# Moving the tiles that transfers touch to the front of the on-chip buffer, each on a multiple of 256 bytes

## The chip, the cores and the metric

One core of a Trainium2 chip runs the kernel. The metric is the device time of one execution in microseconds. The kernel before takes 166.34 us, the median of three runs (165.75 to 167.51 us). The execution that was profiled took 166.82 us, of which 165.1 us lie between its first and its last instruction.

## The reference

The inputs r, k, v and w are arrays of 4 batches, 8 heads, 768 steps and 48 values per head, all float32. An attention with a decaying state runs over the steps, and its output goes through a feed-forward layer with an activation that is normalized twice:

```python
state = zeros((B, H, D, D))
for t in range(S):
    cur = einsum('bhd,bhe->bhde', u * k[t], v[t])
    y[t] = einsum('bhd,bhde->bhe', r[t], state + cur)
    state = w[t][..., None] * state + einsum('bhd,bhe->bhde', k[t], v[t])
x = y, as [3072, 384]
h = x @ w_in                              # 384 x 1024
solu = h * softmax(h)
ln = (solu - mean(solu)) / sqrt(var(solu) + 1e-6) * g_ln
out = ln @ w_out                          # 1024 x 384, float32
```

## The kernel before, in words

The 3072 tokens are cut into 24 units of 128 steps (six chunks of four batches). For each unit four loads bring in 128 rows of w, k, r and v. In memory the 48 float32 values of a step and a head lie side by side, which is 192 bytes, and the rows of a head follow one another; another head lies elsewhere. On chip a row (one partition) of a tile has 8 slots of 64 float32, of which 48 are filled. So a load of 192 KB is made of 1,024 pieces (128 partitions by 8 heads) of 192 bytes each, and the pieces of one partition begin 256 bytes apart. k and r of a unit share a tile `kr_in` of 4,096 bytes a partition; `w_in` and `v_in` have 2,048 each. There are seven buffers of each (`NIO`).

ScalarE then takes the logarithm of w (`lw`), TensorE sums it up over the steps (`cum`), ScalarE takes exponentials (`ex`), VectorE scales k and r (`kp`), TensorE transposes them (`krk`, `krr`), forms the scores (`M`), the output of the attention (`Y`) and the new state (`S`). GpSimd computes the bonus for the step itself (`p`, `q`, `dv`) and casts v (`vb`). The second half transposes y (`X`), multiplies it by w_in (`H`), takes exponential, product and square (`e`, `he`, `hq`), multiplies by w_out (`Oa`, `Ob`; the tile is `o_ps`), scales the rows (`o`) and stores them (`out`, 1,536 bytes a partition).

Both weight matrices are loaded as float32 into `win_f` (three loads of 512 KB) and `wout_f` (two loads of 768 KB, in pieces of 1,536 bytes) and turned into bf16 once. For w_out this is a chain: eight parts are multiplied by the gain (`gw`, seven of them on GpSimd), TensorE takes the column means (`mn`), and VectorE adds them (`ce`; the tile is `w2`, in the rows `w`). Only then can the first `Oa` run.

The order of the work on every engine is the order of the words in the string `ORDER`; each engine follows it strictly (`InOrder`), and so does the queue of SyncE (SP), which issues every load and every store. "hot" are matmuls on a tile of zeros. All instructions are issued by one line of that helper, so in the profile nearly all have line 87, and they are told apart by their tiles.

Tiles in the pool `consts` are allotted in the order in which the code makes them, one behind the other, each rounded up to 32 bytes a partition. Above them lie 16,384 bytes of a scratch area and four constants of 32 bytes each, so the first tile of the kernel begins at byte 16,512 of a partition.

Of the kernel before, what the change touches and what calls it, by code (L numbers as in the profile page):

```python
# [8 lines left out]
F32 = mybir.dt.float32  # L9
# [60 lines left out]
NIO, NLW, NKP, NWK = 7, 10, 6, 4  # L70
# [24 lines left out]
def kernel(  # L95
# [13 lines left out]
    B, H, S, D = r.shape  # L109
    C = 128  # L110
    NC = S // C
    DM = H * D
    DF = moe_w_in.shape[1]
    HP = H // 2
    KM = DM // 128
    KF = DF // 128
# [8 lines left out]
    consts = ctx.enter_context(tc.tile_pool(name="consts", bufs=1))  # L125
    psum = ctx.enter_context(tc.tile_pool(name="psum", bufs=1, space=bass.MemoryType.PSUM))

    def ring(name, n, shape, dtype):
        return [consts.tile(shape, dtype, name=f"{name}{j}") for j in range(n)]
# [2 lines left out]
        return psum.tile(shape, dtype, tag=slot, name=name)  # L132


    warm = consts.tile([128, 512], BF16)
    dve.memset(warm, 0.0)
    uti_neg = consts.tile([C, C], BF16)
# [31 lines left out]
    ones_row = consts.tile([1, C], F32)  # L169
    dve.memset(ones_row, 1.0)  # L170

    w_t = ring("w_in", NIO, [C, H, 64], F32)
    kr_t = ring("kr_in", NIO, [C, 2, H, 64], F32)
    v_t = ring("v_in", NIO, [C, H, 64], F32)
    lw_t = ring("lw", NLW, [C, H, 64], BF16)
    kp_t = ring("kp", NKP, [C, 2, H, 64], BF16)
    for j in range(max(NLW, NKP)):
# [28 lines left out]
    qm_t = ring("qm", NWK, [C, 1], F32)  # L206
    lv_t = ring("lv", NWK, [C, 1], F32)
    rs_t = ring("rs", NWK, [C, 1], F32)
    o_t = ring("o", NWK, [C, DM], F32)

    u_row = consts.tile([1, DM], F32)
    g_rows = consts.tile([KF, 128], F32)
    u_bc = consts.tile([C, H, D], BF16)
    gr = consts.tile([128, KF], F32)
    win_f = consts.tile([128, KM, DF], F32)
    win_sb = consts.tile([128, KM, DF], BF16)
    wout_f = consts.tile([128, KF, DM], F32)
    mean_sb = consts.tile([128, DM], BF16)
    ps = {}

# [274 lines left out]
    def store(i, x):  # L495
# [10 lines left out]
        H=hidden, e=hidden_exp, he=hidden_mul, hq=hidden_square, Oa=output_a, Ob=output_b,  # L506
        sq=sums, qm=variance, lv=scale, o=scaled_out, out=store,
    )
    for word in ORDER.split():
        word, _, how = word.partition(".")  # L510
        name = word.rstrip("0123456789")
# [31 lines left out]
```

## Time and profile before

| what | value |
|---|---|
| median of three runs | 166.34 us |
| profiled execution | 166.82 us, span 165.1 us |
| TensorE (PE) busy | 142.1 us, 86% of the span |
| VectorE (DVE) busy | 130.6 us, 79% |
| ScalarE (ACT) busy | 119.1 us, 72% |
| GpSimd (POOL) busy | 102.7 us, 62% |
| TensorE's granted clock, mean | 0.969 of full |
| transfers | 27.08 MB in 104,825 packets, of which 100,313 under 512 bytes |

"Busy" is the time in which an engine has an instruction under way. The share of the transfer engines is the sum of the durations of all packets over 16 engines and the time; packets of one engine can overlap, so that it can go beyond 100%. SPq is the queue of SyncE: its rows are the times that it took to issue transfers, and waiting for room behind earlier transfers is inside them.

### The profile page before, as it was taken

To read this page: it belongs to the slowest core of one execution; us is meant where nothing else is said; L and a number is where in the kernel's file an instruction comes from. 1 tells how busy PE (TensorE), PEld (TensorE's weight loads), DVE (VectorE), ACT (ScalarE), POOL (GpSimd) and SP (SyncE) were. 2 spreads that over 40 slices of the span, in tenths; PEclk is the share of its full clock that TensorE was granted. 3 is DMA by queue.
4 is the path that set the end of the run, shared out by engine and by line. 5 is a ranking of instruction groups with operands and counts; after the bars stand their busy time and mean duration, and the time that the engine had idled before them with its cause. 6 is when DMAs were issued, how large, how long until landed. Compare 5 with 4: busy or idle time off the path is not lost.

```text
span 165.1 us, 5279 instructions
## 1 busy us (share of the span) xinstructions
PE 142.1 (86%) x2161; PEld 109.8 (67%) x2161; DVE 130.6 (79%) x227; ACT 119.1 (72%) x241; POOL 102.7 (62%) x131
## 2 busy tenths in 40 slices
PE   3789749158799999999999998998899789999990
PEld 1245438027578788887778787785778569798860
DVE  5054668364999999999889987996997899999553
ACT  3162775523779998899988979885979678665951
POOL 7340855996908999697759907999216893770000
PEclk9999999955899999999999999999999999999999
DMA  6999999999999999999999899999999931111023
GB/s 105 167 169 234 195 331 331 148 173 156 168 163 154 182 156 206 139 209 161 171 239 221 140 203 184 201 183 162 189 175 226 183 91 65 38 48 50 1 99 143
DMA packets 104825, 27.08 MB, mean 164 GB/s; under 512 B 100313, under 2 KB 104418, under 8 KB 104802
## 3 DMA queue, kind: packets, MB, share of 16 engines
q1 hardware_dynamic: 104802, 26.75, 92.0%
q8 instruction: 17, 0.28, 0.8%
q14 instruction: 6, 0.05, 0.2%
HBM read 22.03 MB, written 4.72 MB: 162 GB/s over the span
## 4 chain that ended last, share of the span: by engine, by line
PE 33%; DMA 21%; SPq 15%; POOL 10%; DVE 8%; ACT 6%; issue 4%; POOLq 0%; ACTq 0%
SPq L87 15%; PE o_ps L87 12%; PE h_ps L87 9%; DMA w_in<-in_w_dram 6%; DMA kr_in<-in_r_dram 6%; DMA wout_f<-in_moe_w_out_dram 5%; POOL w L87 5%; DMA v_in<-in_v_dram 4%; DVE w L87 3%; PE y_ps L87 3%; PE kr_ps L87 2%; ACT e L87 2%; PE m_ps L87 2%; DVE kp L87 2%; POOL q L87 2%
## 5 line engine op out<-in xcount | busy, mean ns | idle before, releaser
L87 PE MATMUL o_ps<-w,he 128*128 128x385 bf16 x192 | 45.9, 325 | 2.2 <-DVE y L87 1.1
L87 POOL TENSOR_TENSOR p<-kr_in 128x384 bf16<-128x384 f32 x24 | 25.0, 1042 | 23.6 <-DMA kr_in<-in_r_dram 23.5
L87 PE MATMUL h_ps<-xT,win_sb 128*128 128x128 bf16 x576 | 37.0, 223 | 1.5 <-DVE xT L87 1.1
L87 PEld LDWEIGHTS <-win_sb 128*128 128x128 bf16 x576 | 34.3, 100 | 2.4 <-ACT xT L87 1.1
L87 DVE TENSOR_TENSOR he<-h_ps,e 128x1024 bf16<-128x1024 f32 x24 | 29.2, 1218 | 3.8 <-ACT e L87 3.6
L87 PE MATMUL o_ps<-inv_col,e 128*128 128x1 bf16 x192 | 31.7, 165 | 0.0
L87 PE MATMUL o_ps<-one_col,hq 128*128 128x1 bf16 x192 | 31.3, 163 | 0.0
L87 DVE TENSOR_TENSOR kp<-cum_ps,kr_in 128x768 bf16<-128x768 f32 x24 | 22.8, 950 | 9.9 <-ACT cum_ps L87 9.7
L87 ACT ACTIVATE e<-h_ps 128x1024 bf16<-128x1024 f32 x24 | 24.4, 1018 | 7.1 <-PE h_ps L87 7.0
L87 PEld LDWEIGHTS <-hq 128*128 128x128 bf16 x192 | 18.5, 96 | 12.9 <-DVE hq L87 0.2
L87 POOL TENSOR_TENSOR dv<-vb,dg 128x384 bf16<-128x384 bf16 x24 | 20.5, 854 | 7.1 <-DVE dg L87 5.2
L87 POOL TENSOR_TENSOR q<-p,u_bc 128x384 bf16<-128x384 bf16 x24 | 23.2, 970 | 1.1 <-ACT u_bc L87 0.9
L87 ACT ACTIVATE cum_ps<-cum_ps 128x768 f32<-128x768 f32 x24 | 19.3, 804 | 3.2 <-PE cum_ps L87 2.9
L87 PEld LDWEIGHTS <-kp 128*128 128x128 bf16 x272 | 18.0, 101 | 4.0 <-DVE kp L87 1.0
L87 PEld LDWEIGHTS <-e 128*128 128x128 bf16 x192 | 18.4, 96 | 2.9 <-issue 2.5
L87 PE MATMUL kr_ps<-ident,kp 128*128 128x128 bf16 x192 | 19.2, 228 | 0.7 <-DVE xT L87 0.5
L87 PEld LDWEIGHTS <-he 128*128 128x128 bf16 x192 | 18.4, 96 | 1.0
L87 POOL TENSOR_SCALAR_AFFINE_SELECT m<-m 128x1024 bf16<-128x1024 bf16 x14 | 15.3, 1091 | 5.4 <-ACT m L87 3.7
L87 DVE TENSOR_REDUCE dg<-q 128x8 f32<-128x384 bf16 x24 | 12.9, 542 | 3.3 <-POOL q L87 3.3
L87 ACT ACTIVATE lw<-w_in 128x384 bf16<-128x384 f32 x23 | 11.9, 524 | 4.3 <-DMA w_in<-in_w_dram 4.2
L87 ACT CAST m<-m_ps 128x1024 bf16<-128x1024 f32 x14 | 14.2, 1011 | 1.0 <-PE m_ps L87 1.0
L87 PE MATMUL cum_ps<-lw,uti_neg 128*128 128x384 bf16 x24 | 8.7, 361 | 7.0 <-DVE he L87 3.4
(82 smaller groups left out, 280.5 us busy)
## 6 DMA issues: line engine op xcount, KB each, us to landing
w_in<-in_w_dram SPq DMA_DIRECT2D x24, 192.0 KB, 4.9
kr_in<-in_k_dram SPq DMA_DIRECT2D x24, 192.0 KB, 5.1
kr_in<-in_r_dram SPq DMA_DIRECT2D x24, 192.0 KB, 5.4
v_in<-in_v_dram SPq DMA_DIRECT2D x24, 192.0 KB, 5.2
out_dram<-o SPq DMA_DIRECT2D x24, 192.0 KB, 2.6
win_f<-in_moe_w_in_dram SPq DMA_DIRECT2D x3, 512.0 KB, 5.5
wout_f<-in_moe_w_out_dram SPq DMA_DIRECT2D x2, 768.0 KB, 10.5
u_row<-in_u_dram SPq DMA_DIRECT2D x1, 1.5 KB
```

What stands on the lines that cost most here:

```text
L87: made = make(*args, **kwargs)
```

## The change

The nine groups of tiles that transfers write or read are made before all others, behind a pad of 128 bytes that nothing uses. `w_in`, `kr_in`, `v_in`, `win_f`, `wout_f`, `o`, `u_row` and `g_rows` all have sizes that are multiples of 256 bytes, so each then begins at a multiple of 256. The other tiles follow in their old order.

```diff
+    consts.tile([128, 32], F32, name="pad")
+    w_t = ring("w_in", NIO, [C, H, 64], F32)
+    kr_t = ring("kr_in", NIO, [C, 2, H, 64], F32)
+    v_t = ring("v_in", NIO, [C, H, 64], F32)
+    win_f = consts.tile([128, KM, DF], F32)
+    wout_f = consts.tile([128, KF, DM], F32)
+    o_t = ring("o", NWK, [C, DM], F32)
+    u_row = consts.tile([1, DM], F32)
+    g_rows = consts.tile([KF, 128], F32)
...
-    w_t = ring("w_in", NIO, [C, H, 64], F32)
-    kr_t = ring("kr_in", NIO, [C, 2, H, 64], F32)
-    v_t = ring("v_in", NIO, [C, H, 64], F32)
...
-    o_t = ring("o", NWK, [C, DM], F32)
-
-    u_row = consts.tile([1, DM], F32)
-    g_rows = consts.tile([KF, 128], F32)
+
...
-    win_f = consts.tile([128, KM, DF], F32)
...
-    wout_f = consts.tile([128, KF, DM], F32)
```

The addresses that the two programs hold, in bytes from the start of a partition, with the remainder after division by 256:

| first tile of | before | remainder | after | remainder |
|---|---|---|---|---|
| `w_in` (7) | 19,680 | 224 | 16,640 | 0 |
| `kr_in` (7) | 34,016 | 224 | 30,976 | 0 |
| `v_in` (7) | 62,688 | 224 | 59,648 | 0 |
| `win_f` | 190,240 | 32 | 73,984 | 0 |
| `wout_f` | 208,672 | 32 | 86,272 | 0 |
| `o` (4) | 181,248 | 0 | 98,560 | 0 |
| `u_row` | 187,392 | 0 | 104,704 | 0 |
| `g_rows` | 188,928 | 0 | 106,240 | 0 |
| `lw` (10) | 77,024 | 224 | 109,920 | 96 |
| `kp` (6) | 87,264 | 224 | 120,160 | 96 |
| `he` (4) | 164,352 | 0 | 197,248 | 128 |

A piece of 192 bytes that starts at remainder 224 has 32 bytes ahead of the next multiple of 256 and 160 behind it; one that starts at remainder 0 lies inside one stretch of 256. Every engine issues the same instructions in the same order, with the same waits, in both programs; only addresses differ.

## Rows read from the trace of the kernel before

**Rows 1.** The page: span, busy engines, transfer share in 40 slices, packets, queue.
```profile
span 165.1 us, 5279 instructions
...
PE 142.1 (86%) x2161; PEld 109.8 (67%) x2161; DVE 130.6 (79%) x227; ACT 119.1 (72%) x241; POOL 102.7 (62%) x131
...
DMA  6999999999999999999999899999999931111023
...
DMA packets 104825, 27.08 MB, mean 164 GB/s; under 512 B 100313, under 2 KB 104418, under 8 KB 104802
...
q1 hardware_dynamic: 104802, 26.75, 92.0%
```

**Rows 2.** The page: shares of the chain that ended last, by engine and line.
```profile
PE 33%; DMA 21%; SPq 15%; POOL 10%; DVE 8%; ACT 6%; issue 4%; POOLq 0%; ACTq 0%
SPq L87 15%; PE o_ps L87 12%; PE h_ps L87 9%; DMA w_in<-in_w_dram 6%; DMA kr_in<-in_r_dram 6%; DMA wout_f<-in_moe_w_out_dram 5%; POOL w L87 5%; DMA v_in<-in_v_dram 4%; DVE w L87 3%; PE y_ps L87 3%; PE kr_ps L87 2%; ACT e L87 2%; PE m_ps L87 2%; DVE kp L87 2%; POOL q L87 2%
```

**Rows 3.** That chain in order of time, first 45 us: start, duration, what.
```profile
0.79 0.43 SPq L84
...
19.11 8.88 DMA wout_f<-in_moe_w_out_dram
...
28.07 2.47 POOL w L87 x2
...
39.51 4.85 DVE w L87 x7
...
44.40 0.56 PE o_ps L87 x6
```

**Rows 4.** The timeline of SyncE's queue: start, duration, transfer issued.
```profile
7.18 1.20 SPq L87 DMA_DIRECT2D w_in<-in_w_dram  x1
8.43 1.14 SPq L87 DMA_DIRECT2D kr_in<-in_k_dram  x1
```

**Rows 5.** Busy time in three stretches: length, engines, granted clock, DMA share, GB/s.
```profile
28.00:44.40 16.40, 9.95 (x83) 6.50 (x80) 10.12 (x15) 8.75 (x16) 14.62 (x14) 0.69 1.14 164
44.40:80.00 35.60, 35.60 (x602) 29.10 (x602) 34.81 (x58) 31.92 (x69) 27.71 (x33) 1.00 1.04 171
80.00:130.00 50.00, 46.26 (x791) 37.77 (x788) 43.27 (x69) 42.20 (x85) 33.65 (x40) 1.00 1.11 191
```

**Rows 6.** The chain in order of time, 80 to 130 us: its transfers.
```profile
92.74 6.09 DMA v_in<-in_v_dram
...
108.29 6.08 DMA w_in<-in_w_dram
...
122.69 3.87 DMA kr_in<-in_r_dram
```

**Rows 7.** Transfers from 92.5 to 93.5 us: packets, then packets, MB, share.
```profile
DMA packets 1300, 0.25 MB, mean 247 GB/s; under 512 B 1300, under 2 KB 1300, under 8 KB 1300
...
q1 hardware_dynamic: 1300, 0.25, 123.8%
```

**Rows 8.** The same view from 93.75 to 96 us.
```profile
DMA packets 1987, 0.38 MB, mean 167 GB/s; under 512 B 1987, under 2 KB 1987, under 8 KB 1987
...
q1 hardware_dynamic: 1987, 0.38, 141.2%
```

**Rows 9.** The same view from 25 to 26.5 us, while `wout_f` is loaded.
```profile
DMA packets 374, 0.55 MB, mean 365 GB/s; under 512 B 18, under 2 KB 374, under 8 KB 374
...
q1 hardware_dynamic: 374, 0.55, 106.1%
```

**Rows 10.** The same view from 161 to 165 us, with nothing but stores.
```profile
DMA packets 432, 0.59 MB, mean 148 GB/s; under 512 B 48, under 2 KB 432, under 8 KB 432
...
q1 hardware_dynamic: 432, 0.59, 39.5%
```

**Rows 11.** The view of the tile `kr_in`: durations (min/median/max, ns) of `p`.
```profile
L87 POOL TENSOR_TENSOR p<-kr_in x24: 990/999/1463, 6.7 to 135.1; 128x384 bf16<-128x384 f32 x24
```

## The prediction

> **What bounds the kernel now.** I read the page first. TensorE is busy for 142.1 of 165.1 us, and the row of the transfer engines beside it stands at 9 tenths from the second slice to the 32nd [rows 1]. So two things are close to full, and the question for a change that touches only addresses is where transfers come last. Of 104,825 packets 100,313 are under 512 bytes [rows 1]: 24 units by 4 loads by 1,024 pieces are 98,304 of them. The shares of the chain name transfers (21%) and SyncE's queue (15%) beside TensorE (33%) [rows 2].
>
> The chain in order of time says where these shares lie. Up to 19.11 us it is SyncE's queue, then 8.88 us of waiting for `wout_f`; from 28.07 us GpSimd multiplies the gain in, and at 44.40 us the first `o_ps` matmuls run [rows 3]. A plain load takes the queue 1.14 to 1.20 us there [rows 4]. It moves 192 KB, so this is 164 to 172 GB/s: the queue goes as fast as the engines drain it. In the first 28 us the transfer rate therefore sets the end.
>
> From 28 to 44.4 us it is the preparation of w_out (GpSimd busy 14.62 of 16.40 us), with TensorE at 0.69 of its clock on average. From 44.4 to 80 us TensorE is busy for all of 35.60 us and VectorE for 34.81: nothing that a transfer does can shorten that stretch. From 80 to 130 us TensorE has 50.00 - 46.26 = 3.74 us without work [rows 5], and the chain goes through three loads of 6.09, 6.08 and 3.87 us [rows 6]. Behind 130 us nearly all loads are done.
>
> **What the change touches, and the price of a split piece.** No instruction is added, removed or moved. The pieces of w, k, r and v cease to cross a multiple of 256 bytes: 98,304 of 98,304 crossed one before. The weights' pieces (remainder 32) lose one of seven stretches for `wout_f` and one of seventeen for `win_f`. Stores, `u_row` and `g_rows` started at remainder 0 already: nothing, and no cover is needed. Tiles that only engines touch move by multiples of 32 bytes; I cost that at nothing, the last rival says what it would cost otherwise.
>
> No row shows an aligned load of 192 bytes, so I bound its price. The same crossing pieces go at two rates. In one microsecond 1,300 of them passed [rows 7]: 16 engines x 1,000 ns / 1,300 = 12.3 ns per piece and engine. Soon after, 1,987 passed in 2.25 us [rows 8]: 16 x 2,250 / 1,987 = 18.1 ns, while the mean piece lasted 1.412 x 36,000 / 1,987 = 25.6 ns against 1.238 x 16,000 / 1,300 = 15.2 ns. The slow rate is the usual one: 1,024 pieces at 18.1 ns on 16 engines are 1.16 us, the time in the queue's rows [rows 4]. That pieces last longer while fewer pass looks like back-pressure from where they are written or read, not like engines without descriptors; that fast stretches come behind a pause looks like something that fills up.
>
> So the ends are 0 (the crossing is free, since 12.3 ns is reached with it) and 18.1 - 12.3 = 5.8 ns saved per piece (the crossing makes the slow rate). Below 0 I see no reason for a loss in the transfer itself: a piece covers no more stretches than before. Between them lies one more comparison. Packets of 1,536 bytes occur as loads that cross into a seventh stretch and as stores that fill six. With `wout_f` loading, 374 packets took 1.061 x 16 x 1,500 = 25,460 ns; less 18 small ones at 25.6 ns this is 70 ns for each of 356 [rows 9]. Stores: 0.395 x 16 x 4,000 = 25,280 ns, at most 66 ns for each of 384 [rows 10]. The seventh stretch goes with some 4 ns. It compares a load with a store, so it is a loose price, but it is the nearest row, and I take **4.4 ns** of 18.1: a load in the slow state goes from 1.14 to 0.86 us.
>
> [...] The same packets have two rates at one alignment [rows 7, 8], so alignment is not all that counts. [...]
>
> **The sum.**
> - Start. Fifteen loads of 192 KB are issued ahead of `wout_f`. The first three go into empty engines, as in the fast stretch; for twelve I take 1.14 - 0.86 = 0.28 us each, 3.4 us. All of it is on the path to 28.07 us [rows 3, 4], and what follows (GpSimd's gains, VectorE's 4.85 us) only moves up. TensorE was short of work before and after [rows 5], so nothing absorbs it.
> - 28 to 44.4 us: the length stays, since GpSimd sets it. 44.4 to 80 us: full engines, no gain. Next late there would be VectorE and TensorE together.
> - 80 to 130 us: the three transfers in the chain are 16.0 us [rows 6]; 24% of that would be 3.9 us, but TensorE has only 3.74 us without work, and part of that is other engines' doing. I take a third, 1.2 us; ends 0 and 3.7.
> - Behind 130 us: nothing.
>
> Together -4.6 us. The profiled execution took 166.82 us, so 162.2; it lies 0.48 us above the median of the runs (166.34), so the forecast is **161.7 us**.
>
> **The rivals.**
> - *The crossing is free.* What limits pieces of 192 bytes would be their number. For it: 12.3 ns was reached with crossing pieces [rows 7]. Against it: the length of pieces in the slow stretch, 25.6 ns for 192 bytes [rows 8]. The time stays at 166.3 (165.6 to 167.2). [...]
> - *The fast rate everywhere.* If a second stretch per piece is what fills up, 5.8 ns go: a load takes 0.79 us, twelve save 0.35 each, 4.2 us, and the other three half as much, 0.5; the middle gives 3 of its 3.74 us. That is -7.7, 158.6 us. [...]
> - *Slower: engines pay for the new places.* All tiles move, so an engine may meet transfers or another engine in the buffer where it did not before. That durations can depend on such things shows in `p`, which took 990 to 1,463 ns with a median of 999 [rows 11]. The place is VectorE between 44.4 and 130 us, busy for 34.81 + 43.27 = 78.1 us with 0.8 us to spare in the first stretch [rows 5]. 3% on its instructions are 2.3 us: 168.7 us. It decides from some 2.1% (1.66 us) upward, if the loads gain nothing. Against it: shapes, types and multiples of 32 bytes are all as before.
>
> **How the numbers follow.** Forecast 0.42 (159.8 to 165.0, by the ends of its terms), free crossing 0.32, fast rate everywhere 0.18, slower 0.08. A measurement of this kernel tells some 1% from no change: under 164.7 is faster, over 168.0 slower. Of the forecast's cases 0.39 lie under 164.7; with the fast rate that is 0.57. Within 1%: 0.32 of the free crossing, 0.03 of the forecast, together 0.35. Slower: 0.08. The range 157.8 to 167.2 leaves out the slower case and less than half of the fast one; the likeliest case's own range is 159.8 to 165.0.
>
> **What the profile after would show.** Right: plain loads at under 1 us in SyncE's queue before 19 us, a mean rate of 200 GB/s or more where it was 160 to 170, the share of the transfer engines lower at the same bytes, `wout_f` landing near 24.6 us and the first `o_ps` near 41 us, and less idle TensorE between 80 and 130 us. Wrong in the price: the same 1.14 us per load and 28 us for `wout_f`. Wrong in the path: faster loads, but the first `o_ps` not earlier, with GpSimd or VectorE waiting for something that is not a transfer. Slower for the last rival's reason: longer means of `kp`, `he` or `p` at the same count. What would make me wrong above all is a limit in the number of pieces.

## The result, and the profile after

The changed kernel takes 158.01 us, the median of four runs (157.53 to 159.3), against 166.16 us for the kernel before in the same job. The ratio is 0.951, with a 95% interval of 0.943 to 0.959: 5% faster. The profiled execution took 158.2 us, 8.6 us less than that of before. The forecast was 161.7 us in a range of 157.8 to 167.2.

In the experiments below the medians count every execution, while the ratios leave out those over 1.5% above the fastest of their kernel, among them four of 162.5 to 163.0 us (one at remainder 64, one with w and v aligned, two with the stores at 224) of which no run shows the reason.

The page of the kernel after, as in [rows 1, 2]: span, busy engines, transfer share in 40 slices, packets, queue, and the shares of the chain by engine.

```profile
span 156.5 us, 5279 instructions
...
PE 138.6 (89%) x2161; PEld 108.1 (69%) x2161; DVE 129.8 (83%) x227; ACT 118.4 (76%) x241; POOL 103.1 (66%) x131
...
DMA  4999999999999979999559696596999611011024
...
DMA packets 104825, 27.08 MB, mean 173 GB/s; under 512 B 100313, under 2 KB 104418, under 8 KB 104802
...
q1 hardware_dynamic: 104802, 26.75, 75.4%
...
PE 65%; SPq 10%; DVE 9%; POOL 5%; DMA 5%; issue 3%; ACT 1%; DVEq 0%; POOLq 0%
```

The same 104,825 packets take 75.4% of 16 engines where they took 92.0% of a longer span, and transfers have shrunk from 21% to 5% of the chain. TensorE, at 33% before, is now 65% of it.

One stretch of the first loads, 5 to 9 us, in the view of transfers: first the kernel before, then the kernel after (packets; then packets, MB and share of 16 engines).

```profile
DMA packets 3503, 0.66 MB, mean 166 GB/s; under 512 B 3502, under 2 KB 3503, under 8 KB 3503
...
q1 hardware_dynamic: 3503, 0.66, 145.9%
```

```profile
DMA packets 4242, 0.80 MB, mean 201 GB/s; under 512 B 4237, under 2 KB 4242, under 8 KB 4242
...
q1 hardware_dynamic: 4242, 0.80, 103.1%
```

A piece lasted 1.459 x 64,000 / 3,503 = 26.7 ns on average and now lasts 15.6 ns: the long pieces of [rows 8] are gone, and pieces last as long as in the fast stretch of [rows 7]. (In the kernel after, packets take 28.4% of the engines' time in the first half microsecond of this stretch, 5.0 to 5.5 us, and 113.8% from there to 9 us; the rate without a pause is read from the loads by themselves, below.) SyncE's queue shows it per load (start, duration, transfer). In the kernel before, the two loads ahead of those in [rows 4]:

```profile
4.75 1.16 SPq L87 DMA_DIRECT2D v_in<-in_v_dram  x1
5.95 1.19 SPq L87 DMA_DIRECT2D kr_in<-in_r_dram  x1
```

The same four loads in the kernel after:

```profile
5.34 0.59 SPq L87 DMA_DIRECT2D v_in<-in_v_dram  x1
5.97 1.00 SPq L87 DMA_DIRECT2D kr_in<-in_r_dram  x1
7.02 0.99 SPq L87 DMA_DIRECT2D w_in<-in_w_dram  x1
8.05 0.70 SPq L87 DMA_DIRECT2D kr_in<-in_k_dram  x1
```

On average a load took 1.17 us of the queue and now takes 0.82.

The chain of the kernel after in order of time (start, duration, what) answers to [rows 3]:

```profile
17.12 7.74 DMA wout_f<-in_moe_w_out_dram
...
24.95 2.46 POOL w L87 x2
...
36.39 4.85 DVE w L87 x7
...
41.28 0.56 PE o_ps L87 x6
```

The first link to GpSimd comes at 24.95 us in place of 28.07, and all that follows up to the first output matmuls moves with it by 3.12 us and keeps its length. So 3.1 of the 8.6 us are won by 41.28 us. The other 5.5 come later. For the stretch in which they come I take the same work in both: 76.2 to 130.7 us of before and 73.0 to 122.2 us of after (length, engines' busy time, granted clock, DMA share, GB/s), first before, then after.

```profile
76.20:130.70 54.50, 50.76 (x867) 41.48 (x864) 47.69 (x79) 46.14 (x96) 37.09 (x44) 1.00 1.13 191
```

```profile
73.00:122.20 49.20, 49.18 (x869) 41.12 (x868) 47.18 (x79) 45.83 (x96) 37.50 (x43) 1.00 0.82 179
```

54.50 us have become 49.20, which is 5.3 of the 5.5. TensorE's idle time there falls from 3.74 us to 0.02, and its busy time by another 1.58 us for the same matmuls: the ends of matmuls are modelled in this profile, so I read this as waiting that had been covered by "busy". Before it the same matmuls start 3.12 us earlier from 41 to 73 us of the new trace, no more and no less. Behind the stretch nothing more is won.

### The profile page after: what moved, and what is told of

It is laid out like the page before. It is cut to its first block, busy times and chain, and to the rows that moved or that the text cites. A ratio compares the mean times of both kernels' runs of the same rounds, so it can differ in the third digit from the quotient of the medians.

```text
span 156.5 us, 5279 instructions
## 1 busy us (share of the span) xinstructions
PE 138.6 (89%) x2161; PEld 108.1 (69%) x2161; DVE 129.8 (83%) x227; ACT 118.4 (76%) x241; POOL 103.1 (66%) x131
## 2 busy tenths in 40 slices
DMA packets 104825, 27.08 MB, mean 173 GB/s; under 512 B 100313, under 2 KB 104418, under 8 KB 104802
## 3 DMA queue, kind: packets, MB, share of 16 engines
q1 hardware_dynamic: 104802, 26.75, 75.4%
## 4 chain that ended last, share of the span: by engine, by line
PE 65%; SPq 10%; DVE 9%; POOL 5%; DMA 5%; issue 3%; ACT 1%; DVEq 0%; POOLq 0%
PE o_ps L87 23%; PE h_ps L87 17%; SPq L87 10%; PE kr_ps L87 5%; DMA wout_f<-in_moe_w_out_dram 5%; PE s_ps L87 5%; PE y_ps L87 5%; POOL w L87 5%; PE m_ps L87 4%; PE cum_ps L87 3%; DVE w L87 3%; PE x_ps L87 2%; DVE o L87 1%; DVE hq L87 1%; PE mean_ps L87 1%
## 5 line engine op out<-in xcount | busy, mean ns | idle before, releaser
L87 PE MATMUL h_ps<-xT,win_sb 128*128 128x128 bf16 x576 | 36.5, 222 | 0.7 <-DVE xT L87 0.7
L87 DVE TENSOR_TENSOR he<-h_ps,e 128x1024 bf16<-128x1024 f32 x24 | 29.2, 1217 | 3.1 <-ACT e L87 2.7
L87 POOL TENSOR_TENSOR p<-kr_in 128x384 bf16<-128x384 f32 x24 | 24.5, 1023 | 10.9 <-DMA kr_in<-in_r_dram 10.9
L87 PEld LDWEIGHTS <-hq 128*128 128x128 bf16 x192 | 18.5, 96 | 12.8
L87 POOL TENSOR_TENSOR q<-p,u_bc 128x384 bf16<-128x384 bf16 x24 | 23.7, 990 | 1.6 <-DMA kr_in<-in_k_dram 1.5
L87 PEld LDWEIGHTS <-kp 128*128 128x128 bf16 x272 | 17.5, 99 | 3.9 <-DVE kp L87 1.2
L87 PE MATMUL kr_ps<-ident,kp 128*128 128x128 bf16 x192 | 18.7, 225 | 0.9 <-DVE xT L87 0.5
L87 ACT COPY kr<-kr_ps 128x1024 bf16<-128x1024 bf16 x10 | 10.1, 1014 | 4.1 <-PE kr_ps L87 4.1
L87 DVE TENSOR_TENSOR m<-m_ps,keep 128x1024 bf16<-128x1024 f32 x10 | 12.1, 1215 | 0.9 <-PE m_ps L87 0.9
```

The source lines that it names most:

```text
L87: made = make(*args, **kwargs)
```

## The experiments

All kernels are one core; "before" is the kernel before in the same job. Theories: *crossing* (a piece that runs over a multiple of 256 bytes pays for a second write), *start* (a piece pays for the bytes between its start and the multiple below), *places* (alignment of the transfers is not it; other tiles' places are).

### The input tiles at other remainders, in the changed layout

Two pads around the input tiles shift them alone; every other tile keeps the remainder that it has in the change. For remainder 224:

```diff
-    consts.tile([128, 32], F32, name="pad")
+    consts.tile([128, 88], F32, name="pad")
...
     v_t = ring("v_in", NIO, [C, H, 64], F32)
+    consts.tile([128, 8], F32, name="pad_back")
```

At 64 the two pads have 48 elements each, at 96 they have 56 and 40, at 128 they have 64 and 32.

> The changed layout with one edit: w_in, kr_in and v_in start at remainder 224 again; all other tiles keep the remainders of the change. Crossing theory (a piece that runs over a multiple of 256 pays for a second write): the whole gain goes, 166 us, mean piece near 20.6 ns, plain loads 1.1 us in the queue. Start theory (a piece pays for the bytes between its start and the multiple of 256 below): the same, 166 us. Places theory (the gain comes from where the engines' own tiles or the weights now lie): the gain stays, 158 us.

> The input tiles at remainder 64: a piece of 192 bytes ends exactly at the next multiple of 256, so it crosses none, but it does not start on one. Crossing theory: 158 us, every piece 15 ns as in the change. Start theory in its strict form (any start off the grid is slow): 166 us. [...] Places theory: 158 us.

> The input tiles at remainder 96: a piece has 160 bytes before a multiple of 256 and 32 behind it. Crossing theory: 166 us, as at 224. [...] Places theory: 158 us.

> The input tiles at remainder 128: 128 bytes before a multiple of 256 and 64 behind it, both whole multiples of 64. Crossing theory: 166 us. [...] A variant (only a part that is no multiple of 64 bytes is slow to write): 158 us here, while 96 and 224 are slow. Places theory: 158 us.

In this job the kernel before takes 165.43 us.

| remainder | crosses | median us | ratio to before (95%) |
|---|---|---|---|
| 64 | no | 158.58 | 0.956 (0.948 to 0.963) |
| 96 | yes | 165.29 | 0.996 (0.992 to 1.001) |
| 128 | yes | 163.85 | 0.992 (0.988 to 0.995) |
| 224 | yes | 165.1 | 0.997 (0.993 to 1.001) |

The queue's row on the pages of the four kernels, in the order 64, 96, 128, 224 (packets, MB, share of 16 engines):

```profile
q1 hardware_dynamic: 104802, 26.75, 75.5%
```

```profile
q1 hardware_dynamic: 104802, 26.75, 92.8%
```

```profile
q1 hardware_dynamic: 104802, 26.75, 94.3%
```

```profile
q1 hardware_dynamic: 104802, 26.75, 90.3%
```

What counts is whether the piece crosses. At 64 it starts off the grid and ends on the next line, and all of the gain is there. At 96 it has only 32 bytes behind the line, and the gain is gone. Neither the start theory (at 96 a piece would pay for 96 bytes where it pays for 224 before, and lose less) nor its strict form (64 should be slow) survives, nor the variant on multiples of 64 bytes (128 should be fast); 128 is 0.8% better than before, which I can't explain. With 224 all other tiles and the weights lie as in the change and the gain is gone: the places carry none of it that these runs can tell.

How wide the stretches are is shown from one side only. A grid of 128 or 64 bytes is ruled out: at remainder 128 a piece touches as many such stretches as at 0, and it is slow. A grid of 512 is not ruled out by these remainders: the pieces begin 256 bytes apart, so where all of them cross a multiple of 256, every second one crosses a multiple of 512. The loads by themselves come back to this.

### The old layout with the input tiles aligned, whole and half

```diff
+    consts.tile([128, 8], F32, name="pad")
     w_t = ring("w_in", NIO, [C, H, 64], F32)
     kr_t = ring("kr_in", NIO, [C, 2, H, 64], F32)
     v_t = ring("v_in", NIO, [C, H, 64], F32)
+    consts.tile([128, 56], F32, name="pad_back")
```

> The layout of before, with one edit: two pads (32 and 224 bytes) put w_in, kr_in and v_in at remainder 0. Order of the tiles, weights at remainder 32, all other remainders as before. Crossing theory: all of the gain, 158 us. If the new places of the weights or of the engines' tiles carried a part of it, the time stays above: the control at 224 leaves at most 0.5 us for them, so 158 to 158.5 us.

Measured: 158.53 us against 166.98, ratio 0.952 (0.947 to 0.957). Two pads in the old order do all of it; that the weights end at remainder 32 costs nothing that shows.

For the half, pads of 8 and 56 elements stand around `w_in` and around `v_in`, and `kr_in` keeps 224:

```diff
+    consts.tile([128, 8], F32, name="pad")
     w_t = ring("w_in", NIO, [C, H, 64], F32)
+    consts.tile([128, 56], F32, name="pad_back")
     kr_t = ring("kr_in", NIO, [C, 2, H, 64], F32)
+    consts.tile([128, 8], F32, name="pad2")
     v_t = ring("v_in", NIO, [C, H, 64], F32)
+    consts.tile([128, 56], F32, name="pad_back2")
```

> The layout of before with only w_in and v_in at remainder 0; kr_in stays at 224, so half of the pieces cross. Crossing theory with a price for each crossing: the mean piece halfway (near 18 ns), a start gain of half (1.5 us) and a time near 162 us. If the slow state is a state of the whole transfer path that any crossing pieces bring about, the pieces of w and v are slow too, and the time stays at 165 to 166 us.

Measured: 159.1 us, ratio 0.953 (0.949 to 0.957), not to be told from the whole alignment. Both forms of the expectation failed: half of the pieces still cross and next to nothing is lost. The queue's row on the page of this kernel:

```profile
q1 hardware_dynamic: 104802, 26.75, 79.0%
```

79.0% lies near the 75.4% of the change, not halfway to 92.0%. So a crossing has no fixed price; the last experiment measures that by itself.

### The stores at remainder 224, in the changed layout

```diff
+    consts.tile([128, 56], F32, name="pad_o")
     o_t = ring("o", NWK, [C, DM], F32)
+    consts.tile([128, 8], F32, name="pad_back")
```

> The changed layout, but the output tiles o at remainder 224: each stored row of 1,536 bytes is read over seven stretches of 256 in place of six. My loose price in the prediction (4 ns for a seventh stretch) would make a store packet 69 ns instead of 65; 24 x 128 packets on 16 engines are 0.8 us of engine time at most, off the path until the last stores: 158.0 to 158.3 us. If crossing costs only where the buffer is written and not where it is read, packets stay at 65 ns and the time at 158.0.

Measured: 158.91 us, ratio 0.951 (0.946 to 0.956), beside 158.53 and 159.1 us of the two kernels above in the same job. The two forms of the expectation are too near to each other to be told apart by time, but the packets part them. The view of transfers over the last 4.5 us, with little but stores in it, first for the change (152.0 to 156.5 us), then for this kernel (156.5 to 161.0 us; packets, then packets, MB and share of 16 engines):

```profile
DMA packets 434, 0.59 MB, mean 131 GB/s; under 512 B 49, under 2 KB 434, under 8 KB 434
...
q1 hardware_dynamic: 434, 0.59, 35.2%
```

```profile
DMA packets 437, 0.60 MB, mean 132 GB/s; under 512 B 49, under 2 KB 437, under 8 KB 437
...
q1 hardware_dynamic: 437, 0.60, 37.3%
```

The packets took (0.373 - 0.352) x 16 x 4,500 = 1,512 ns more. Less three packets of 65 ns that only the second view holds, this is some 3.4 ns for each of its 388 stored rows. So a row that is read over a seventh stretch lasts longer, by about the 4 ns of the first form, in the one execution that was profiled (162.84 us). In the kernel's time it does not show.

### The change with w_out loaded later

```diff
-krr0 cum2.b0 LV2 kr0.d hot1.s3 LO0 M0.b1 krr1 LO1 m0.d hot3.s3 kr1.a LW4 LK4 p2 et0 ex2 M1.b1 LR4 hot4.s3 LW5
+krr0 cum2.b0 LV2 kr0.d hot1.s3 M0.b1 krr1 m0.d hot3.s3 kr1.a LW4 LK4 p2 et0 ex2 M1.b1 LR4 hot4.s3 LW5 LO0 LO1
```

> The change, with the two loads of w_out issued four loads later (behind LW4 LK4 LR4 LW5): this takes away the head start of 3.1 us at the first output matmul and leaves the faster loads. If the gain in the middle (5.5 us between 76 and 131 us of before) comes from the faster loads there, it stays, and the time is 158 + 3 = 161 us. If it grew out of the head start, both go and the time is 164 to 166 us. If the later stretches take up the delay, 158 to 159 us.

Measured: 163.65 us, ratio 0.982 (0.977 to 0.987). This lies between the forms of the expectation (161, and 164 to 166), so the time alone decides nothing. The delay was larger than I had counted. In the view of SyncE's queue (start, duration, transfer) the four loads ahead hold the queue from 17.00 to 23.71 us, two of them for 2.75 and 1.87 us, so that w_out is issued at 23.71 us, 6.6 us later than in the change (17.12):

```profile
18.33 2.75 SPq L87 DMA_DIRECT2D kr_in<-in_k_dram  x1
21.12 1.87 SPq L87 DMA_DIRECT2D kr_in<-in_r_dram  x1
...
23.71 1.26 SPq L87 DMA_DIRECT2D wout_f<-in_moe_w_out_dram  x2
```

The view of the tile `o_ps` gives the start of the first and the last of 192 output matmuls (durations min/median/max, first to last start). First before, then after, w_out late, w and v alone:

```profile
L87 PE MATMUL o_ps<-w,he x192: 323/324/338, 42.8 to 160.4; 128*128 128x385 bf16 x192
```

```profile
L87 PE MATMUL o_ps<-w,he x192: 323/324/338, 38.7 to 151.8; 128*128 128x385 bf16 x192
```

```profile
L87 PE MATMUL o_ps<-w,he x192: 323/324/338, 44.5 to 157.5; 128*128 128x385 bf16 x192
```

```profile
L87 PE MATMUL o_ps<-w,he x192: 323/324/337, 39.3 to 152.4; 128*128 128x385 bf16 x192
```

From first to last these are 117.6, 113.1, 113.0 and 113.1 us. With w_out late the first output matmul even starts 1.7 us later than before, and the stretch behind it is as short as in the change. So the gain in the middle doesn't need the head start. A later start also gives the loads more time to get ahead, but in the change the outputs start 4.1 us earlier than before, and the stretch is as short: what is left for it is the faster loads. (The control at 224 runs from 41.4 to 158.4 us, 117.0: the long stretch is back with the crossing. In single traces of the others it is 114.7 us at 96, 116.0 at 128 and 112.1 at 64. The control's start is 1.4 us earlier than that of before in this one execution, so the start of a single trace is good to some 1.4 us.)

### The loads by themselves

These four kernels leave out all of the computation: 96 loads one behind the other, then 24 stores of zeros. Only the pads between the input tiles differ, as above.

```diff
-    for word in ORDER.split():
-        ...
+    for i, (c, b) in enumerate(units):
+        sp.dma_start(out=w_t[i % NIO][:, :, :D], in_=rows_of(w))
+        sp.dma_start(out=kr_t[i % NIO][:, 0, :, :D], in_=rows_of(k))
+        sp.dma_start(out=kr_t[i % NIO][:, 1, :, :D], in_=rows_of(r))
+        sp.dma_start(out=v_t[i % NIO][:, :, :D], in_=rows_of(v))
```

> Leaves out all of the computation: the 96 loads of w, k, r and v one behind the other, then 24 stores of zeros. No piece crosses. It gives the pace that the engines reach by themselves. In the change the queue took 0.70 us for a load, so 10.9 to 12.3 ns a piece: 67 to 76 us for the loads.

> The same with w_in at remainder 224: one load in four is made of crossing pieces. Two-limits theory (a piece goes at the engines' pace, or at 9.05 ns for each stretch that it touches on a path behind them that has a store of its own, whichever is slower on average): 1.25 x 9.05 = 11.3 ns a piece, so at most 4% more than without crossing. Price theory (a crossing costs some 6 to 7 ns wherever it occurs): 12.5 to 13 ns, some 15% more.

> The same with kr_in at remainder 224 and w_in and v_in at 0: half of the pieces cross, as in the kernel that aligned w and v alone. Two-limits theory: 1.5 x 9.05 = 13.6 ns a piece, 84 us for the loads. Price theory: halfway between none and all, 14.5 to 15.2 ns, 89 to 93 us.

> The same with all input tiles at remainder 224. Both theories: 18.1 ns a piece as in the slow stretch of before, 111 us for the loads. If the loads run at the pace of the first kernel without any engine working beside them, the limit lies in the transfers' own path; if they are as fast as without crossing, the engines' use of the buffer is part of it.

The view of transfers from 10 to 90 us of each, in the order none, a quarter, half, all (packets, MB, rate):

```profile
DMA packets 88345, 16.72 MB, mean 209 GB/s; under 512 B 88344, under 2 KB 88344, under 8 KB 88344
```

```profile
DMA packets 87460, 16.55 MB, mean 207 GB/s; under 512 B 87459, under 2 KB 87459, under 8 KB 87459
```

```profile
DMA packets 85285, 16.14 MB, mean 202 GB/s; under 512 B 85284, under 2 KB 85284, under 8 KB 85284
```

```profile
GB/s 163 164 163 163 164 163 163 163 163 164 163 163 164 163 163 163 163 163 163 163 163 163 163 163 163 163 163 164 163 163 164 163 163 163 163 163 163 163 163 163
DMA packets 69067, 13.06 MB, mean 163 GB/s; under 512 B 69067, under 2 KB 69067, under 8 KB 69067
```

The queue's rows in the same views and order (packets, MB, share of 16 engines):

```profile
q1 hardware_dynamic: 88344, 16.71, 106.2%
```

```profile
q1 hardware_dynamic: 87459, 16.54, 105.4%
```

```profile
q1 hardware_dynamic: 85284, 16.13, 109.5%
```

```profile
q1 hardware_dynamic: 69067, 13.06, 149.8%
```

| pieces that cross | ns per piece and engine (16 x 80,000 / packets) | price theory, linear between the ends | a piece lasts, ns (share x 16 x 80,000 / packets) | execution, us |
|---|---|---|---|---|
| none | 14.5 | 14.5 | 15.4 | 107.2 |
| a quarter | 14.6 | 15.5 | 15.4 | 108.05 |
| half | 15.0 | 16.5 | 16.4 | 110.76 |
| all | 18.5 | 18.5 | 27.8 | 132.6 |

The four points fit two limits, of which the slower one sets the pace. Crossing everywhere gives a flat 163 GB/s in each of the 40 slices, 18.5 ns per piece or 9.3 ns for each stretch of 256 bytes that it touches. Without crossing something else sets 14.5 ns. At half, 1.5 x 9.3 = 13.9 ns is still under that, and 15.0 is measured, so the passage from one limit to the other is not sharp. By the figures written down beforehand, half would have gone to the price theory (14.5 to 15.2 ns); what speaks against that theory are the ends as measured, 14.5 and 18.5, which put a half at 16.5 and a quarter at 15.5. On a grid of 512 bytes, all crossing would be 1.5 stretches a piece, 18.5 / 1.5 = 12.3 ns for each, and the half could not take less than 1.25 x 12.3 = 15.4 ns. 15.0 speaks for 256, but it is one run and near. My figure for the faster limit was too low (12.3 ns, read from one microsecond behind a pause, in which packets took 7.9% of the engines' time from 91 to 91.5 us and 11.5% from 91.5 to 92; 14.5 over 80 us), the kind was right. Three quarters weren't tried. No engine computes here, so the long pieces (27.8 ns) belong to the path of the transfers, not to engines that use the buffer beside them. Each kernel of this group ran once.

## Why the prediction was right, and where its sizes were off

**What bounds the kernel** was read rightly: the transfers up to the gains of w_out, nothing from 44.4 us to near 80, transfers again up to 130 us. The head start is constant over the full stretch, 3.12 us.

**The price of a split piece**: 4.4 ns were taken, between ends of 0 and 5.8. The loads alone give 18.5 - 14.5 = 4.0 ns when all pieces cross. The size was right, in part by luck, since the reason given for it was another: I took what a seventh stretch adds to the length of one packet from a load beside a store (the stores at 224 give 3.4 ns for that), and by the four points what the loads pay is not a price per crossing but the distance of two limits. Of the three things that I read in the rows, two hold: the long pieces of the slow stretch come from the writing side, since they go (26.7 ns before, 15.6 after) when the addresses written to are the only thing that changes, and alignment is not all that counts (15.0 ns with half of the pieces crossing, 14.5 with none). What fills up behind a pause, and what sets 14.5 ns, no run shows.

**The start**: -3.4 us forecast, -3.1 us by the chain. The signs named for it came: loads at 0.59 to 1.00 us in the queue, 0.82 on average where 0.86 was forecast; 201 GB/s in place of 166; the first output matmul in the chain at 41.28 us where I wrote near 41. But 3.1 is the difference of one pair of traces. The link to GpSimd, at 28.07 us before and 24.95 after, comes at 27.34 and 27.38 us in the chains of the kernels at 96 and 128, and at 25.29 and 26.35 in those at 64 and with the input tiles alone aligned. So the start is worth 1 to 3 us, and the near match with 3.4 is partly luck.

**The middle** is the term that was mis-sized: -1.2 us with ends of 0 and 3.7, against -5.5. Three things were wrong in that step. I took 24% off the transfers in the chain and then a third of that. But here the savings added up over all the loads that are queued one behind the other, and with the transfers ahead of the work the waits went whole: the chain of after has no transfer behind `wout_f`, and TensorE's idle time in the middle is 0.02 us. I also left out two loads of that chain that begin before 80 us, because TensorE is full there (35.60 of 35.60 us, [rows 5]):

```profile
62.77 5.90 DMA kr_in<-in_r_dram
...
74.80 4.23 DMA w_in<-in_w_dram
```

With them the chain's transfers from 44.4 to 130 us are 26.2 us in place of 16.0. So here a late load in a stretch in which TensorE is full was still in the chain of what follows. And I took TensorE's idle time, 3.74 us, for the most that there was to win; its busy time fell by another 1.6 us, by my reading waiting that it had hidden. That bound was no bound.

**28 to 44.4 us** and **behind 130 us**: nothing was forecast and nothing measured.

**The rivals.** *Free crossing* fell with the control at 224 and with the loads alone, though it holds up to half of the pieces. *The fast rate everywhere* gave 158.6 us, and the time came out there; its terms were 4.7 us at the start and 3 in the middle, so it has the sum for a different split. *Slower by the new places*: the means of `p` (1,042 before, 1,023 ns now), `kp` (950 and 948) and `he` (1,218 and 1,217) did not grow, and `p` has the spread of [rows 11] at the new places too; what makes it, no run shows. Its view (min/median/max):

```profile
L87 POOL TENSOR_TENSOR p<-kr_in x24: 993/1000/1465, 5.7 to 126.4; 128x384 bf16<-128x384 f32 x24
```

That the time fell below the forecast's own range of 159.8 to 165.0 is the middle's doing. That range does not follow from the ends of its terms either: 0 to 4.7 us at the start and 0 to 3.7 in the middle make 157.9 to 166.3. The wider range that I stated, 157.8 to 167.2, holds 158.01 us by 0.2 us, through the part of the fast rival that it takes in and not through the forecast.

**The bytes ahead of a piece's start** are not what is paid for here: 96 was as slow as 224 (165.29 and 165.1 us), and 64 kept the gain (158.58 us). A load for which 0.86 us were forecast takes 0.93 us in the loads alone without crossing (1,024 x 14.5 ns / 16) and 1.18 us with all pieces crossing (1,024 x 18.5 ns / 16).

## What to carry to other kernels

Where many short pieces are written to the buffer, try a place for the tile at which no piece runs over a multiple of 256 bytes: for 192-byte pieces this took 166.16 us to 158.01. They did not have to start on one (158.58 us at remainder 64), and it was enough that half of them did not cross (159.1 us). Look for a flat transfer rate (here 163 GB/s in the loads alone) with pieces that last longer than the same pieces elsewhere in the trace (25.6 ns against 15.2, [rows 7, 8]). And when transfers are the pace over a long stretch, count what is saved on every one of them, not a share of the waits that happen to stand in the chain, and don't take an engine's idle time for the most that can be won: here it was 3.74 us, and 5.3 were won.

## What was not expected of the hardware

- Half of the pieces crossed at next to no cost: 15.0 ns a piece against 14.5 with none and 18.5 with all, and 159.1 us for the whole kernel against 158.5.
- With all pieces crossing the rate is flat at 163 to 164 GB/s, slice by slice over 80 us, with nothing else running; without crossing it is higher, at 209 GB/s on average.
- 32 bytes behind the line cost as much as 160: 165.29 us at remainder 96 and 165.1 us at 224.
- Stored rows that are read over seven stretches in place of six lasted longer in the one execution that was profiled, by some 3.4 ns of 65 (37.3% against 35.2% of the engines' time in the last 4.5 us), which the kernel's time does not show.
